# Moving the operands of an expert layer to other distances modulo 512 bytes

## The chip, the cores and the metric

One core of a Trainium2 chip runs the whole program. The metric is the device time of one execution in microseconds; a time of several runs is their median. SBUF, the on-chip memory from which TensorE reads, has 128 partitions, and a tile has one byte address that holds in each of them. "Modulo 512" below means that address modulo 512 bytes.

## The reference, cut to what matters

```python
def _attn_ref(q, k, v, s):                     # B, H, S, D = 8, 8, 576, 64
    scores = q @ k.T / sqrt(D)                 # causal, with a bias from the running sum of relu(s)
    ...
    return softmax(scores) @ v

def _moe_ref(x, modality_id, w_gate, modality_bias, w1, w2):
    e_idx = np.argmax(x @ w_gate + modality_bias[modality_id], axis=1)      # one of 8 experts a row
    ...
    for e in range(E):                         # x 4608 x 512, w1 512 x 1024, w2 1024 x 512
        mask = e_idx == e
        h = np.maximum(x[mask] @ w1[e], 0.0)
        out[mask] = gate_w[mask, None] * (h @ w2[e])
```

The output of attention, turned so that one row is one position with all heads, is the input of a layer with eight experts, of which each row uses one.

## The kernel before, in words

**Attention** (`Attn`, until about 365 us) goes through 32 pairs of heads. For each it makes score tiles from QH, QL (loaded operand) and KA, KB (streamed operand) at lines 374, 396, 409 and 410, takes exponentials, turns the tiles on TensorE against an identity (`ident`, lines 441 and 456) and multiplies with V (line 528). Its tiles lie in pools of their own, which are given back before the expert stage needs the room.

**Routing** (`Route`) writes the rows of each expert to a list in memory.

**The expert stage** (`Moe`, from about 368 us) takes blocks of 256 rows of one expert: 18 blocks by `block`, then by `two` a closing block of two 64-row pieces of different experts. For each block:

- `fetch` starts the transfer of a chunk of 512 KB of the expert's weights into a raw buffer, `wraw` (2 buffers) or `wrbw` (4 buffers); an expert has 8 chunks, four of w1 and four of w2.
- `parts` splits a chunk into a high and a low part (ScalarE or GpSimd copies the high part, VectorE or GpSimd subtracts) and writes both into a tile of 2 x 1024 columns: `wca` (4 buffers), `wcb` (5) or `wcc0` to `wcc3` (4), used in rotation.
- `gather2` loads the rows, `xt` turns them and splits them into `xT`, 2 x 4 x 256 columns, two buffers. The first block's turned rows are made during attention, in a buffer of attention's that still stands (`early_rows`), and show in the profile under the name `x`.
- `block` computes the first layer (line 1198): 96 matmuls that load 128 columns of a weight tile and stream 256 columns of `xT`. It writes the activations, split again, into `hT`. `second` computes the second layer (line 1172): 48 matmuls that load 128 columns of `hT` and stream 512 columns of a weight tile.

A matmul's loaded operand shows in the profile under PEld (LDWEIGHTS), the matmul itself under PE. TensorE takes them in the order of the program.

**Where tiles lie.** A pool gives its tiles room in the order in which their names are first asked for, and a pool begins where the one before it ends; the pool of `wcc` stands on the right side and is filled downwards from its end. `gap` asks for a tile that nothing uses; it only moves what stands after it (in the pool of `wcc`, what stands before it). The order is: `mwa` (`wraw` x2, then `wca` x4), then attention's constant tiles or, after attention, `mys` (ys), `mmx` (xr, tg, xg), `mwr` (`wrbw` x4), `mwb` (gap, `wcb` x5), `mm` (gap, three `oi` of 32 bytes, `hT` of 16384 bytes, `xT` x2 of 8192 bytes each), `mtb`. `mwa` begins at 22176, `wraw` at 160 modulo 512.

Of the kernel before, what the change touches and what calls it, by code (L numbers as in the profile page):

```python
# [8 lines left out]
F32R = mybir.dt.float32r  # L9
# [8 lines left out]
P = 128  # L18
# [643 lines left out]
class Route:  # L662
# [82 lines left out]
    def group(self, bp, x, psum, mm, then=None):  # L745
# [5 lines left out]
        for g in range(3):  # L751
            t = slice(4 * g, min(4 * g + 4, 9))
            nc.vector.tensor_reduce(out=lg[:, t].rearrange("p t (d r) -> p t d r", r=2), in_=x[g][:, :, 32:].rearrange("p t d h r -> p t d r h"), axis=AX.X, op=ALU.add)
            yield True
        nc.vector.tensor_tensor(lg, lg, self.mbs[:, 9 * bp:9 * bp + 9], ALU.add)
        mx = w.tile([P, 9], F32, name="rmx")
        nc.vector.tensor_reduce(out=mx, in_=lg, axis=AX.X, op=ALU.max)
        yield True
# [7 lines left out]
        nc.vector.scalar_tensor_tensor(oh, lg, 0.0, self.ew.unsqueeze(1).broadcast_to(B3), ALU.is_equal, ALU.mult)  # L766
        nc.vector.tensor_reduce(out=mx, in_=oh, axis=AX.X, op=ALU.max)
        gs = w.tile([P, 9], F32, name="gs")
        yield True
        ohb = self.ohb[bp % 2]  # L770
        nc.vector.tensor_tensor(ohb[:, :9], oh, mx.unsqueeze(2).broadcast_to(B3), ALU.is_equal)
        nc.vector.tensor_reduce(out=gs, in_=ex, axis=AX.X, op=ALU.add)
        for _ in range(2 if mm else 0):
# [28 lines left out]
        df = pt[:, 60:69]  # L802
        nc.vector.tensor_reduce(out=df, in_=pos, axis=AX.X, op=ALU.add)
        nc.vector.tensor_copy(di, df)
# [27 lines left out]
    def spread(self, tag, n, E, nb):  # L832
# [23 lines left out]
        def pick(v, name):  # L856
            r = cell(nb, name)
            if v is None:
                nc.vector.tensor_reduce(out=r, in_=oh, axis=AX.X, op=ALU.add)
            else:  # L860
# [123 lines left out]
class Moe:  # L984
    def __init__(self, ctx, tc, R, w1, w2, ident, out):
        self.nc, self.tc, self.R, self.w1, self.w2, self.ident, self.out = tc.nc, tc, R, w1, w2, ident, out
        self.wa = ctx.enter_context(tc.tile_pool(name="mwa", bufs=1))
        self.wb = None
        self.n = 0
        self.last = [None] * 4  # L990
        self.hold = None
        self.late, self.stop = None, 1 << 30
        self.back = ()
        self.er = None
        self.conv, self.high = [], None

    def open(self, ctx):
        tc = self.tc
        self.my, self.mx, self.wr, self.wb, self.mp = (
            ctx.enter_context(self.tc.tile_pool(name=n, bufs=2, reuse_waits="tile")) for n in ("mys", "mmx", "mwr", "mwb", "mm"))  # L1000
        self.R.tb = ctx.enter_context(tc.tile_pool(name="mtb", bufs=1, reuse_waits="tile"))
        self.ps = ctx.enter_context(tc.tile_pool(name="mps", bufs=2, space=PSUM, reuse_waits="tile"))
        self.gap(self.wb, 416)
        self.gap(self.mp, 96)

    def gap(self, pool, n):
        pool.tile([P, n // 4], F32, name="gap", bufs=1)
# [1 line left out]
    def open2(self, ctx):  # L1009
        self.wc = ctx.enter_context(self.tc.tile_pool(name="mwc", bufs=1, reuse_waits="tile", side="right"))  # L1010
        for n in ("ql", "hs"):
            self.wc.tile([P, 512], F32, name=n, bufs=2)
        for i in range(self.NC):
            self.wc.tile([P, 2, 1024], F32R, name=f"wcc{i}")
        self.gap(self.wc, 320)

    NA, NB, NC = 4, 5, 4

# [18 lines left out]
    def parts(self, raw, d, n, j, w=None):  # L1037
        nc = self.nc
        m = (n - self.NA) % (self.NA + self.NB + self.NC)
        if w is not None:  # L1040
            pass
        elif n < self.NA or self.NB <= m < self.NB + self.NA:
            w = self.wa.tile([P, 2, 1024], F32R, name="wca", bufs=self.NA)
        elif m < self.NB:
            w = self.wb.tile([P, 2, 1024], F32R, name="wcb", bufs=self.NB)
        else:
            w = self.wc.tile([P, 2, 1024], F32R, name=f"wcc{(m - self.NB - self.NA + 2) % self.NC}")
        n += 1
        with ExitStack() as after:
            for i in self.tr[1:] if 4 < n <= 8 else self.back:  # L1050
                after.enter_context(self.tc.issue_after(i.ins))
            if n <= self.NA:
                nc.gpsimd.tensor_scalar(w[:, 0], raw, 1.0, 1.0, ALU.mult, ALU.mult)
            else:
                self.high = nc.scalar.copy(w[:, 0], raw).ins
            self.conv.append((self.high, (nc.gpsimd if n in WGP else nc.vector).tensor_tensor(w[:, 1], raw, w[:, 0].bitcast(F32), ALU.subtract).ins))
        return w, d
# [19 lines left out]
    def weights2(self, es):  # L1077

        W = [], []

        def more():
            for j in range(8):
                for q in range(2):
                    w = None
                    if (j, q) == (6, 1):
                        w = self.mp.tile([P, 2, 4, 256], F32R, name="xT").rearrange("p a k n -> p a (k n)")
                    w, d = self.parts(*self.fetch(es[q], j), w)
                    W[q].append(w)
                    self.hold = d.ins
                    yield  # L1090
        return W, more()
# [48 lines left out]
    def xt(self, xg, nu):  # L1140
        nc = self.nc
        if nu < 2:
            return self.xq(xg) if nu else self.x2(xg)
        xT = self.mp.tile([P, 2, 4, 256], F32R, name="xT")
        for g in range(2):
            tp = self.ps.tile([P, 2, 256], F32, name="tp")
            tr = nc.vector.transpose(out=tp.rearrange("p k (t n) -> p k t n", n=32),
                                     in_=xg[0].rearrange("p t (d k) -> p k t d", k=4)[:, 2 * g:2 * g + 2])
            hi = nc.scalar.copy(xT[:, 0, 2 * g:2 * g + 2], tp)
            lo = nc.vector.tensor_tensor(xT[:, 1, 2 * g:2 * g + 2], tp, xT[:, 0, 2 * g:2 * g + 2].bitcast(F32), ALU.subtract)  # L1150
        self.tr = (tr, hi, lo)
        return xT
# [57 lines left out]

    def xq(self, xg):
        nc = self.nc
        xT = self.mp.tile([P, 2, 4, 256], F32R, name="xT")[:, 0, :, :P]
        tp = self.ps.tile([P, 4, 64], F32, name="tp")
        for k in range(4):
            nc.tensor.transpose(out=tp[:, k], in_=self.quads(xg[:64], k), identity=self.ident[:64, :64])
        nc.scalar.copy(xT[:, :, :64], tp)
        nc.vector.tensor_tensor(xT[:, :, 64:], tp, xT[:, :, :64].bitcast(F32), ALU.subtract)
        return xT
# [12 lines left out]

    def x2(self, xg):
        nc = self.nc
        X = self.mp.tile([P, 2, 4, 256], F32R, name="xT")[:, 0]
        tp = self.ps.tile([P, 4, P], F32, name="tp")
        for k in range(4):
            nc.tensor.transpose(out=tp[:, k], in_=self.quads(xg, k), identity=self.ident)
        self.split(X, tp)
        return X  # L1240

    def sums2(self, o, W, parts, scale=1.0, after=(), apart=False):

        nc = self.nc
        n = len(parts)
        def order(i):
            return (0, 1) if i == 0 else (1, 0)

        if apart:

            seq = [(i, c, q) for h in range(2) for q in range(2) for i in range(n // 2 * h, n // 2 * h + n // 2) for c in order(i)]
        else:
            seq = [(i, c, q) for i in range(n) for c in order(i) for q in range(2)]
        for i, c, q in seq:
            x, k, c0 = parts[i]
            m = 64 if c else P
            self.last[0] = nc.tensor.matmul(o[q][:m], x[:, P * q:P * q + m], W[q][k][:, c, c0:c0 + 512], start=i == 0 and c == 0, stop=i == n - 1 and c == 0)
        lo = self.wc.tile([P, 512], F32, name="ql", bufs=2)
        for q in range(2):
            with ExitStack() as behind:  # L1260
                for i in after:
                    behind.enter_context(self.tc.issue_after(i.ins))
                r = slice(64 * q, 64 * q + 64)
                self.last[3] = nc.scalar.activation(lo[r], o[q][64:], AF.Copy, scale=scale if type(scale) is float else scale[r])
        return lo
# [287 lines left out]
```

## Time and profile before

| | |
|---|---|
| median of the runs shown | 791.98 us (791.36 to 792.59, 2 runs) |
| the profiled execution | 791.26 us |
| its span, first to last instruction | 789.5 us |
| instructions | 17275 |
| mean granted clock of TensorE | 0.997 |
| matmuls (PE) / loads (PEld) | 5796 / 5796 |

A group of instructions is shown with its line, engine, operation, the tiles it writes and reads, its shape (loaded rows\*columns, then streamed rows x columns), its count, its busy time and the mean duration of one. Matmuls overlap in the pipeline and their ends are modelled, so the duration of one is longer than the time to the start of the next; that time is called the pitch below. A table by stretches gives, for each engine, the busy time and the number of instructions, then the granted clock, the share of the transfer engines that is busy, and GB/s.

### The profile page before, as it was taken

How to read it: one execution, taken by the hardware profiler on the slowest of the kernel's cores; microseconds unless marked ns; L12 is line 12 of the kernel's file. 1: busy time of each engine (PE TensorE's matmuls, PEld its weight loads, DVE VectorE, ACT ScalarE, POOL GpSimd, SP SyncE). 2: the span in 40 equal slices, each digit the busy share in tenths (PEclk: the TensorE clock that was granted, in tenths of full speed). 3: DMA queues.
4: the chain of work that ended last, by engine and by line, in shares of the span. 5: the costliest groups of instructions: out<-in, count | busy, mean ns of one | idle time of the engine just before them, and what ended most of it. 6: DMA issues, size and time to landing. Idle time of an engine off the chain costs nothing. (4 is left out here: it accounts for less than half of the span.)

```text
span 789.5 us, 17275 instructions
## 1 busy us (share of the span) xinstructions
PE 774.3 (98%) x5796; PEld 673.1 (85%) x5796; DVE 568.3 (72%) x1440; ACT 518.4 (66%) x1163; POOL 367.1 (46%) x386
## 2 busy tenths in 40 slices
PE   7999999999999999998999999999999999999996
PEld 6888788888888888887888999999999998999984
DVE  7675577665766666777689797877777776778664
ACT  6887878878888778884455445655555555455553
POOL 8978877898789978994610101110000011001011
PEclk9999999999999999999999999999999999999999
DMA  7467556776567765757888979877788787887750
GB/s 241 132 225 224 186 191 190 216 249 215 157 185 236 230 194 155 233 181 237 272 305 278 329 240 335 241 266 243 244 265 270 256 245 249 267 264 266 269 171 29
DMA packets 88168, 181.21 MB, mean 230 GB/s; under 512 B 13785, under 2 KB 33113, under 8 KB 87950
## 3 DMA queue, kind: packets, MB, share of 16 engines
q1 hardware_dynamic: 82238, 160.03, 65.1%
q0 software_dynamic: 5840, 20.06, 6.6%
q8 instruction: 46, 0.75, 0.4%
q14 instruction: 44, 0.36, 0.2%
HBM read 143.59 MB, written 26.80 MB: 216 GB/s over the span
## 5 line engine op out<-in xcount | busy, mean ns | idle before, releaser
L1184 POOL DMA_INDIRECT out<-ys,oi x36 | 40.8, 1132 | 339.5 <-ACT ys L1183 245.8
L421 ACT ACTIVATE pe<-pe,mx 128x512 f32<-128x512 f32 (+3 forms) x256 | 142.4, 559 | 11.7 <-DVE mx L398 11.6
L398 DVE CUSTOM_DVE_ANT_0 pe<-sp,mk 128x512 f32<-128x512 f32 (+3 forms) x256 | 116.6, 481 | 43.2 <-ACT rs L538 20.2
L445 ACT COPY PT<-pt 128x512 f32<-128x512 f32 (+1 forms) x192 | 94.3, 504 | 27.4 <-PE pt L441 26.4
L441 PE MATMUL pt<-ident,pe 128*128 128x128 f32 x640 | 106.1, 278 | 0.9 <-ACT PT L445 0.7
L374 PE MATMUL sp<-KA,QH 128*128 128x256 f32 (+2 forms) x256 | 98.1, 388 | 1.8 <-POOL KA L238 1.8
L1200 ACT ACTIVATE hT<-hp 128x512 fp32r<-128x512 f32 x72 | 43.1, 599 | 85.2 <-PE hp L1198 85.0
L328 POOL TENSOR_TENSOR QL<-rawq,QH 64x576 fp32r<-64x576 f32 x62 | 87.0, 1422 | 0.3
L328 POOL TENSOR_TENSOR KA<-rawk,KA 64x576 fp32r<-64x576 f32 x62 | 86.4, 1412 | 0.1
L1198 PE MATMUL hp<-xT,wcb 128*128 128x256 f32 x648 | 86.1, 277 | 0.0
L441 PEld LDWEIGHTS pt<-ident,pe 128*128 128x128 f32 x640 | 77.2, 144 | 9.0 <-ACT PT L445 2.0
L396 PE MATMUL sp<-KB,QL 76*128 76x256 f32 (+2 forms) x256 | 83.8, 329 | 1.1 <-DMA KB<-KA 0.9
L528 PE MATMUL o<-PT,V 128*64 128x512 f32 (+1 forms) x496 | 84.5, 440 | 0.0
L1198 PEld LDWEIGHTS hp<-xT,wcb 128*128 128x128 f32 x648 | 79.9, 188 | 0.8 <-DVE hT L1201 0.2
L1201 DVE SCALAR_TENSOR_TENSOR hT<-hp,hT 128x512 fp32r<-128x512 f32 x72 | 49.5, 687 | 41.8 <-ACT hT L1200 41.4
L1172 PE MATMUL y<-wcb,hT 128*128 128x512 f32 x336 | 79.3, 392 | 0.0
L1172 PEld LDWEIGHTS y<-wcb,hT 128*128 128x128 f32 x336 | 62.5, 188 | 13.1
L1198 PE MATMUL hp<-xT,wca 128*128 128x256 f32 x528 | 72.3, 277 | 0.0
L1198 PEld LDWEIGHTS hp<-xT,wca 128*128 128x128 f32 x528 | 66.0, 188 | 0.7 <-DVE hT L1201 0.2
L528 PEld LDWEIGHTS sp<-PT,V 128*64 128x64 f32 x620 | 38.2, 137 | 33.3 <-issue 28.8
L1198 PE MATMUL hp<-xT,wcc 128*128 128x256 f32 x456 | 63.0, 277 | 1.1 <-DVE hT L1201 1.1
L1172 PE MATMUL y<-wca,hT 128*128 128x512 f32 x264 | 62.3, 392 | 0.0
(300 smaller groups left out, 1688.0 us busy)
## 6 DMA issues: line engine op xcount, KB each, us to landing
wrbw<-in_w SPq DMA_DIRECT2D x104, 512.0 KB
wraw<-in_w SPq DMA_DIRECT2D x56, 512.0 KB
rawq<-in_qkv SPq DMA_DIRECT2D x31, 576.0 KB
rawk<-in_qkv SPq DMA_DIRECT2D x31, 576.0 KB
V<-in_qkv SPq DMA_DIRECT2D x32, 320.0 KB
KB<-KA SPq DMA_DIRECT2D x62, 144.0 KB
xr<-lists SPq DMA_DIRECT2D x68, 128.0 KB
lists<-z SPq DMA_DIRECT2D x8, 576.0 KB
```

The lines of the kernel that those rows point to most:

```text
L328: self.last = nc.gpsimd.tensor_tensor(o, i, h, ALU.subtract).ins
L374: self.pe.append(self.nc.tensor.matmul(sp[:, :nn], QH[:, q0:q0 + P], self.KA[u][:, ab, :nn], start=True, stop=False).ins)
L396: self.pe.append(nc.tensor.matmul(sp[:, :nn], QL[:EXT, q0:q0 + P], KB[:EXT, ab, :nn], start=False, stop=True).ins)
L398: ins = nc.vector.tensor_tensor_reduce(out=t[:, :n], in0=sp[:, :n], in1=self.mk[:, 512 - n:512], scale=-0.125, scalar=3.0e38, op0=ALU.add, ...
L421: self.act = nc.scalar.activation(t[:, :n], t[:, :n], AF.Exp, bias=m, scale=-1.0, accum_out=st["sums"][:, o:o + 1]).ins
L441: self.pe.append(nc.tensor.transpose(out=pt[:, o:o + P], in_=pe[:, P * j:P * j + P], identity=self.ident).ins)
L445: return cp(w[:, :, :, v:v + P], pt[:, :n * (1 + both)].rearrange("p (a j q) -> p a j q", a=1 + both, q=P))
L528: m = nc.tensor.matmul(t[r, q0 - b:q1 - b], V[:, ab, j, :], PT[:, ab, PTS * j + q0 if j < 4 else PTW - 64:PTS * j + q1 if j < 4 else PTW], ...
L1172: self.last[0] = nc.tensor.matmul(y[u], hT[:, a, f, P * u:P * u + P], W[4 + f // 2][:, c, 512 * (f % 2):512 * (f % 2) + 512], start=f == 0 ...
L1198: nc.tensor.matmul(hp[:, u], W[k][:, a, f:f + P], xT[:, c, k], start=k == 0 and i == 0, stop=k == 3 and i == 2)
L1200: hi = nc.scalar.activation(hs, hp, AF.Relu)
L1201: lo = nc.vector.scalar_tensor_tensor(hT[:, 1, 2 * m:2 * m + 2], hp, 0.0, hs.bitcast(F32), ALU.max, ALU.subtract)
```

## The change

Every tile of the expert stage that TensorE reads is moved:

- a gap of 224 bytes before the first `wca`, which also moves everything behind the pool `mwa` by 224 bytes;
- the gap before `wcb` grows from 416 to 480 bytes;
- the gap ahead of `hT` grows from 96 to 192 bytes;
- the gap in the pool of `wcc` grows from 320 to 384 bytes;
- `xT` becomes a tile of 2176 columns (8704 bytes), and the 2048 columns in use begin at column 32 or at column 40, in turn, that is 128 or 160 bytes into the tile.

```diff
@@ Moe.__init__
+        self.nx = 0
@@ Moe.open
-        self.gap(self.wb, 416)
-        self.gap(self.mp, 96)
+        self.gap(self.wb, 480)
+        self.gap(self.mp, 192)
+
+    def turned(self):
+        t = self.mp.tile([P, 2176], F32R, name="xT")
+        self.nx += 1
+        o = 32 + 8 * (self.nx % 2)
+        return t[:, o:o + 2048].rearrange("p (a k n) -> p a k n", a=2, k=4)
@@ Moe.open2
-        self.gap(self.wc, 320)
+        self.gap(self.wc, 384)
@@ Moe.parts
         elif n < self.NA or self.NB <= m < self.NB + self.NA:
+            if n == 0:
+                self.gap(self.wa, 224)
             w = self.wa.tile([P, 2, 1024], F32R, name="wca", bufs=self.NA)
@@ Moe.weights2
-                        w = self.mp.tile([P, 2, 4, 256], F32R, name="xT").rearrange("p a k n -> p a (k n)")
+                        w = self.turned().rearrange("p a k n -> p a (k n)")
@@ Moe.xt (and likewise xq and x2)
-        xT = self.mp.tile([P, 2, 4, 256], F32R, name="xT")
+        xT = self.turned()
```

The number and the order of the instructions in the source, their shapes and their buffers' counts are the same.

More of the change, by code (lines that the diff above doesn't have):

```diff
@@ L1212, in xq @@
         nc = self.nc
-        xT = self.mp.tile([P, 2, 4, 256], F32R, name="xT")[:, 0, :, :P]
+        xT = self.turned()[:, 0, :, :P]
         tp = self.ps.tile([P, 4, 64], F32, name="tp")
@@ L1234, in x2 @@
         nc = self.nc
-        X = self.mp.tile([P, 2, 4, 256], F32R, name="xT")[:, 0]
+        X = self.turned()[:, 0]
         tp = self.ps.tile([P, 4, P], F32, name="tp")
```

## The prediction

> **What bounds the kernel now.** I read the page from the top: busy times first, then the slices.
>
> ```profile
> PE 774.3 (98%) x5796; PEld 673.1 (85%) x5796; DVE 568.3 (72%) x1440; ACT 518.4 (66%) x1163; POOL 367.1 (46%) x386
> PE   7999999999999999998999999999999999999996
> ```
>
> TensorE is busy from the second slice to the last but one. The table by stretches confirms it for the expert stage (420 to 740 us), and the list of TensorE's waits says how little is left to win by ending a wait:
>
> ```profile
> 420.00:740.00 320.00, 318.91 (x2091) 289.50 (x2091) 249.49 (x334) 176.69 (x226) 32.57 (x29) 1.00 0.82 263
> ...
> PE hp L1198 <- DVE hT L1201: 1.9, 3, 0.9
> PE sp L374 <- POOL KA L238: 1.8, 1, 1.8
> ```
>
> 318.91 of 320 us are busy at a granted clock of 1.00 (third column from the end), and the longest wait sums to 1.9 us over the whole span. No row in that list waits for a weight or for a turned row. So this stage's length is the number of its matmuls times their pitch, the time from one start to the next. Only something that alters the pitch, or makes an operand late, can move the end.
>
> The pitch is read from the timeline, which merges neighbours: start, length, group, count. One whole expert block, with the end of the block before it:
>
> ```profile
> 447.49 0.84 PE L1198 MATMUL hp<-xT,wcc 128*128 128x256 f32 x6
> 448.17 5.66 PE L1172 MATMUL y<-wcc,hT 128*128 128x512 f32 x24
> 453.66 5.66 PE L1172 MATMUL y<-wcb,hT 128*128 128x512 f32 x24
> 459.15 1.21 PE L1198 MATMUL hp<-xT,wcb 128*128 128x256 f32 x9
> ...
> 470.06 2.22 PE L1172 MATMUL y<-wca,hT 128*128 128x512 f32 x9
> ```
>
> The 48 second-layer matmuls start from 448.17 to 459.15: 10.98 us, 228.8 ns each. The 96 first-layer matmuls start from 459.15 to 470.06: 10.91 us, 113.6 ns each. A block is 21.9 us and there are 18. By line, with shortest, median and longest duration:
>
> ```profile
> L1198 PE MATMUL hp<-xT,wcb x648: 276/276/384, 392.3 to 755.7; 128*128 128x256 f32 x162
> L1198 PE MATMUL hp<-xT,wca x528: 276/276/385, 392.6 to 756.0; 128*128 128x256 f32 x176
> L1198 PE MATMUL hp<-xT,wcc x456: 276/276/384, 414.5 to 734.1; 128*128 128x256 f32 x152
> L1198 PE MATMUL hp<-x,wca x96: 276/276/384, 368.1 to 381.2; 128*128 128x256 f32 x96
> L1172 PE MATMUL y<-wcb,hT x336: 388/392/400, 381.3 to 745.0; 128*128 128x512 f32 x168
> L1172 PE MATMUL y<-wca,hT x264: 388/392/477, 403.5 to 764.7; 128*128 128x512 f32 x132
> L1172 PE MATMUL y<-wcc,hT x264: 388/392/394, 406.2 to 767.4; 128*128 128x512 f32 x132
> ```
>
> These are 1728 first-layer and 864 second-layer matmuls. A duration here is the pitch plus a fixed tail: 276 - 113.6 = 162 and 392 - 228.8 = 163 ns. So durations can be compared across lines as pitches. Price of a nanosecond: 1728 + 864 = 2592 matmuls, 2.6 us.
>
> **The change part by part.** It adds no instruction and removes none; tiles move. I add up the sizes in order of allocation. Before, all weight tiles (wca, wcb, wcc) begin at 160 modulo 512 bytes, and hT, xT and the first block's turned rows at 352. Every column offset used (128 or 256 floats) is a multiple of 512, so in the first layer the streamed operand lies 192 past the loaded one, and in the second 320. After: wca 160 + 224 = 384; wcb 160 + 224 + 64 = 448; wcc 64 lower, 96; hT 448 + 96 + 192 = 736, that is 224; xT's data at 224 + 128 = 352 and 224 + 160 = 384 in turn. The distances become 480 and 0 (wca), 416 and 448 (wcb), 256 and 288 (wcc) in the first layer, 160, 224 and 384 in the second: nine, so it does what it says.
>
> *First and second layer.* What does a distance cost? The weights of the next matmul load while this one streams, so the pair to judge is one matmul's streamed and the next one's loaded operand. At the joints of a block other tiles meet. The last first-layer matmul streams xT (352) while hT (352) loads: distance 0. The six starts from 447.49 to 448.17 take 0.68 us, 113.3 ns each, that joint included, against 113.6 at 192. The last y streams a chunk while the next chunk loads, again 0, inside the 228.8. So distance 0 costs less than the timeline's 10 ns rounding in a joint, and the shortest and median durations give no line a second level.
>
> The attention scores meet other distances: within a row of QH, KA, QL, KB these are 0, 64, 128, 256 and 384, with a little of 192 and 320 where another line follows.
>
> ```profile
> L410 PE MATMUL sp<-KB,QL x128: 292/297/442, 15.8 to 353.1; 76*128 76x288 f32 x128
> L456 PE MATMUL pt<-ident,pep x128: 270/273/330, 21.5 to 359.3; 128*128 128x128 f32 x128
> ```
>
> L410 (64, 256 and 384) has shortest and median 5 ns apart: one level again. L456 turns tiles in two buffers 2304 bytes apart, so it sees 32 and 288 already, and its shortest and median are 270 and 273: no second level. L410's pitch is 297 - 163 = 134 ns for 288 columns, 0.465 a column, where the first layer has 113.6 / 256 = 0.444. That is the one sign in the trace that another distance may be dearer; those matmuls also use 76 rows and wait for and release other engines. 160, 224, 416, 448 and 480 are not judged by any of these rows.
>
> If halving the loaded operand shortened the pitch, the load and the stream would be in each other's way. In the closing block the same line does both:
>
> ```profile
> L1257 PE MATMUL hp<-wcc,hT 128*64 128x512 f32 x6 | 2.4, 393 | 0.0
> L1257 PE MATMUL hp<-wcc,hT 128*128 128x512 f32 x6 | 2.4, 392 | 0.0
> ```
>
> 393 ns with 64 columns before, 392 with 128: at 320 there is nothing to win. I cost the pitch at nothing. Bounds: below, every matmul at its line's shortest, 392 - 388 = 4 ns on 864, and 0 on the first layer, whose median is its shortest: -3.5 us. Above, all at L410's price a column: (0.465 - 0.444) x 256 = 5.4 ns x 1728 = 9.3 us, and for the second layer (0.465 x 512 - 228.8) = 9.3 ns x 864 = 8.0 us, +17.3 us together. I take 0, the value nearest to the joints, which are these same lines.
>
> By the Trainium skill's page "TensorE: Matmul & The Clock Gate", section "Back-to-back issue gap", a warm gap would be N / 2.4 + 2.5, which is 109.2 and 215.8 ns; by that figure an estimate of 4.4 x 1728 + 13.0 x 864 = 18.8 us could be won at most, and the trace stands above it everywhere.
>
> *Splitting, turning, raw weights.* ACT, DVE and POOL read and write moved tiles. The two raw buffers stand at different distances from the chunk (wraw 0, wrbw 96) before:
>
> ```profile
> L1056 DVE TENSOR_TENSOR wca<-wraw,wca x16: 1211/1218/1227, 387.5 to 762.2; 128x1024 fp32r<-128x1024 f32 x16
> ...
> L1056 DVE TENSOR_TENSOR wca<-wrbw,wca x32: 1198/1219/1228, 388.6 to 767.9; 128x1024 fp32r<-128x1024 f32 x32
> ```
>
> 1218 and 1219 ns: no price. What hides it if there is one: TensorE's list holds no wait for a chunk, and DVE is busy 249 of 320 us; 70 us of slack for some 130 such operations, half a microsecond each.
>
> *Transfers.* wrbw moves from 256 to 480 modulo 512, xr from 160 to 384; wraw stays at 160. Waits of the converting engines for each, before:
>
> ```profile
>   DMA wraw<-in_w: 2.5, 4
> ...
>   DMA wrbw<-in_w: 1.7, 2
> ```
>
> 56 chunks to 160 and 104 to 256 waited 2.5 and 1.7 us in all, and no matmul behind them did. Cost 0; bound: the stage's transfer share of 0.82 could rise by a fifth before transfers set the pace.
>
> The Trainium skill's page "DMA: Bandwidth & Descriptors", section "How a descriptor splits into AXI transactions", speaks against this part: a piece that does not begin on 256 bytes needs a transaction more. By it wrbw's 4096-byte rows would need 17 in place of 16, an estimate of 6% on 104 of 160 chunks, a share near 0.85, and still no matmul late, so the sum is the same by both.
>
> *Attention.* Its tiles all move by 224, so their mutual distances stay; only the identity (unmoved) meets pe at 320 instead of 32, and L456 shows two such distances alike. 0, bound 3 ns on 800 turnings, 2.4 us.
>
> *Sum.* 0. The profiled execution took 791.26 us for a span of 789.5, 1.8 around it; the median shown is 791.98. I predict 792.0.
>
> **The rivals.**
>
> *A load that no longer hides (slower).* At wca's distances, 0 and 480, load and stream run over nearly the same addresses modulo 512; if they excluded each other, the load would come on top. The price is read from the turnings, where a 128-column stream is too short to hide a load:
>
> ```profile
> 200.33 0.60 PE L441 MATMUL pt<-ident,pe 128*128 128x128 f32 x4
> ```
>
> 0.60 less the last one's 0.272, over 3, is 109 ns, against 57 for half of a first-layer matmul: 52 ns exposed. On half of wca's 528 (distance 0), 13.7 us: 806. On all 528 and the first block's 96, 32 us: 824. It decides from 300 matmuls on, where 52 ns make 15.8 us. Against it: the joint at 0. For it: a joint is one matmul in 96, and 480 is unseen.
>
> *All distances but 192 and 320 are dearer.* L410's price: 809; half of it: 800.
>
> *Faster.* The nine distances could remove part of what stretches the matmuls. The rows alone give -3.5 us, 788.5; the whole of the skill's gap would be 773. Against it: the 64-column rows.
>
> *It does not do what it says.* The pools could round or order tiles otherwise than I added up; then some distances stay and the time is 792 again.
>
> **How the numbers follow.** No change, 788 to 796: 0.70. Addresses otherwise, also 792: 0.05. All dearer, 797 to 809: 0.13, a fifth of it past 2%. Load exposed, 806 to 824: 0.08, four fifths of it past 2%. Faster: 0.04, of which 0.02 past 2%. A kernel's measurement tells about 2% (15.8 us) from no change. Faster by over 2%: 0.02; slower by over 2%: 0.03 + 0.06 = 0.09; the rest, 0.89, within. The range goes from 786, under the rows' bound of 788.5, to 807, under the top of the dearer case; most of the exposed case stays out.
>
> **What would show it.** Right: L1198 at 276 and L1172 at 392 median for all of wca, wcb and wcc, and the stretch 420 to 740 with about 2091 matmuls. Exposed load: wca's median in L1198 near 300 or in two levels, wcb's and wcc's unmoved. All dearer: 282 and 401 in all lines. Late weights: TensorE waits for a chunk, which it now never does. Wrong beyond that: a level at 160 or 224 in the second layer, where no row warned.

## The result, and the profile after

The changed kernel takes 802.52 us (801.90 to 803.15, 2 runs) against 791.98: a ratio of 1.0132, 95% interval 1.0114 to 1.015. The profiled execution took 801.9 us for a span of 800.2, 10.7 us longer than before's 789.5. Ratios here and below are of fast executions alone, which leaves out one of e2's four, at 1972.08 us. The top of the page after:

```profile
PE 785.7 (98%) x5796; PEld 681.3 (85%) x5796; DVE 569.3 (71%) x1440; ACT 518.3 (65%) x1163; POOL 364.6 (46%) x386
```

PE's busy time rose by 11.4 us for the same 5796 matmuls and that of their loads by 8.2; DVE, ACT and POOL moved by 2.5 us at most. The table by stretches says where (busy time and count of PE, PEld, DVE, ACT, POOL, then granted clock, transfer share, GB/s):

```profile
0.00:368.00 368.00, 360.50 (x3114) 300.97 (x3114) 249.02 (x1008) 290.22 (x869) 312.14 (x339) 1.00 0.65 204
368.00:420.00 52.00, 51.88 (x333) 47.25 (x334) 39.08 (x61) 27.62 (x41) 15.39 (x13) 0.97 0.86 264
420.00:740.00 320.00, 319.15 (x2049) 288.32 (x2048) 246.96 (x331) 171.43 (x220) 31.73 (x29) 1.00 0.80 261
```

In the expert stretch TensorE is as busy as before (319.15 us) and gets 2049 matmuls done in place of 2091, at a clock of 1.00 in both. It is not waiting; each matmul is longer. The transfer share fell from 0.82 to 0.80 with the pace. The 0.97 in the second row is a stretch of 3.4 us at half clock, about 1.7 us of time; the profiles below have none, one or two such stretches there, and before's other executions range from 0.992 to 0.999 in mean granted clock, so I don't count it into the change's price.

By line, with shortest, median and longest duration:

```profile
L1207 PE MATMUL hp<-xT,wcb x648: 276/281/287, 393.8 to 766.1; 128*128 128x256 f32 x162
L1207 PE MATMUL hp<-xT,wca x528: 274/282/302, 394.1 to 766.4; 128*128 128x256 f32 x176
L1207 PE MATMUL hp<-xT,wcc x456: 274/281/384, 416.4 to 743.9; 128*128 128x256 f32 x152
L1207 PE MATMUL hp<-x,wca x96: 277/281/588, 369.1 to 382.4; 128*128 128x256 f32 x96
L1181 PE MATMUL y<-wcb,hT x336: 388/395/398, 382.6 to 755.0; 128*128 128x512 f32 x168
L1181 PE MATMUL y<-wca,hT x264: 390/397/479, 405.2 to 775.2; 128*128 128x512 f32 x132
L1181 PE MATMUL y<-wcc,hT x264: 387/393/408, 408.0 to 778.0; 128*128 128x512 f32 x132
```

The median of the first layer went from 276 to 281 or 282 for every weight tile, that of the second from 392 to 393, 395 and 397. The timeline shows it as pitch:

```profile
449.88 0.87 PE L1207 MATMUL hp<-xT,wcc 128*128 128x256 f32 x6
450.59 5.73 PE L1181 MATMUL y<-wcc,hT 128*128 128x512 f32 x24
456.16 5.76 PE L1181 MATMUL y<-wcb,hT 128*128 128x512 f32 x24
461.75 1.22 PE L1207 MATMUL hp<-xT,wcb 128*128 128x256 f32 x9
```

48 starts from 450.59 to 461.75 are 11.16 us, 232.5 ns each (228.8 before); the six from 449.88 are 0.71 us, 118 ns each (113.3 before). The list of TensorE's waits holds nothing new in the expert stage; its one row there is:

```profile
PE hp L1207 <- DVE hT L1210: 0.7, 1, 0.7
```

Adding up the time from each start to the next over all recorded matmuls: first layer 199.3 to 206.6 us (+7.3), second layer 198.5 to 201.8 (+3.4), everything else 391.8 and 391.8. So the whole loss lies in the two lines whose operands moved.

To judge each distance I matched the recorded starts to the program's matmuls with their two addresses (streamed operand of one, loaded operand of the next) and took the mean of start to next start within a layer:

| layer | before | after, by distance |
|---|---|---|
| first, 256 columns | 192: 113.8 ns | 0: 119.3; 256: 118.8; 288: 117.0; 416: 118.3; 448: 116.1; 480: 118.3 |
| second, 512 columns | 320: 229.1 ns | 160: 234.1; 224: 233.1; 384: 232.5 |

Weighted by count that is +4.1 ns on 1728 and +4.2 ns on 864: 7.1 + 3.6 = 10.7 us. (The half clock adds 1.7 us to the first layer; shorter waits for hT, 1.9 to 0.7 us, take 1.2 from it; that the sum meets the span to a tenth is partly chance.) All nine are dearer, and over these distances the two layers pay about the same per matmul.

### The profile page after: what moved, and what is told of

It reads as the page before. It is cut to its first block, busy times and chain, and to the rows that moved or that the text cites. A ratio compares the mean times of both kernels' runs of the same rounds, so it can differ in the third digit from the quotient of the medians.

```text
span 800.2 us, 17275 instructions
## 1 busy us (share of the span) xinstructions
PE 785.7 (98%) x5796; PEld 681.3 (85%) x5796; DVE 569.3 (71%) x1440; ACT 518.3 (65%) x1163; POOL 364.6 (46%) x386
## 5 line engine op out<-in xcount | busy, mean ns | idle before, releaser
L1193 POOL DMA_INDIRECT out<-ys,oi x36 | 39.1, 1086 | 350.8 <-ACT ys L1192 256.9
L1207 PE MATMUL hp<-xT,wcb 128*128 128x256 f32 x648 | 88.1, 280 | 0.0
L1207 PEld LDWEIGHTS hp<-xT,wcb 128*128 128x128 f32 x648 | 81.8, 188 | 0.6
L1207 PE MATMUL hp<-xT,wca 128*128 128x256 f32 x528 | 74.9, 282 | 0.0
L1207 PEld LDWEIGHTS hp<-xT,wca 128*128 128x128 f32 x528 | 68.4, 190 | 0.5
L1207 PE MATMUL hp<-xT,wcc 128*128 128x256 f32 x456 | 64.8, 281 | 0.8 <-DVE hT L1210 0.7
```

The costliest lines, as they stand in the source:

```text
L1207: nc.tensor.matmul(hp[:, u], W[k][:, a, f:f + P], xT[:, c, k], start=k == 0 and i == 0, stop=k == 3 and i == 2)
```

## The experiments

All edits are against the kernel before. Where xT moves within its tile (not in e1, and otherwise in e4), it does so by the change's own function with one start column for both buffers:

```diff
+    def turned(self):
+        t = self.mp.tile([P, 2176], F32R, name="xT")
+        o = ...                                # the column given with the experiment
+        return t[:, o:o + 2048].rearrange("p (a k n) -> p a k n", a=2, k=4)
```

**Is it the place or the distance?** e1_all_moved moves weights (to 384), xT and hT (to 64), the first block's rows and the raw buffer wrbw (to 480) and keeps the distances at 192 and 320.

```diff
+            if n == 0:
+                self.gap(self.wa, 224)
-        self.gap(self.wc, 320)
+        self.gap(self.wc, 96)
-        xT = b[:, 32:2080]...
+        xT = b[:, 88:2136]...
```

> Every expert tile is moved as far as or further than in the change (weights 160 to 384, turned rows and hT 352 to 64, wrbw 256 to 480, attention's tiles by 224), but all distances stay at 192 and 320. Theory D (the pitch depends on the distance between the streamed and the loaded operand alone): 792 us, first layer 113.8 ns, second 229.1 ns a matmul. Rival A (where an operand itself lies, or the moved raw buffers and their transfers, cost the time): about 801 us, pitches near 118 and 233. Rival V (it is the variety of distances, not their values): 792 us.

Measured: 791.76 us, ratio 0.9987 (0.9977 to 0.9997). Its row of the stretches and two of its groups (busy time and mean ns behind the bar):

```profile
420.00:740.00 320.00, 318.91 (x2092) 289.43 (x2091) 249.93 (x334) 176.84 (x226) 33.06 (x29) 1.00 0.82 264
```

```profile
L1200 PE MATMUL hp<-xT,wcb 128*128 128x256 f32 x648 | 85.9, 277 | 0.0
...
L1174 PE MATMUL y<-wcb,hT 128*128 128x512 f32 x336 | 79.2, 391 | 0.0
```

2092 matmuls in the stretch against 2091, 277 and 391 ns. Absolute places, transfers into a raw buffer at 480, splitting and turning cost nothing that shows; if anything the kernel is 1 us faster. The Trainium skill's page "DMA: Bandwidth & Descriptors", section "How a descriptor splits into AXI transactions", would by the prediction's reading have given wrbw's rows one transaction more (the page tells it of the bytes that a transaction fetches, and wrbw is written). The share stands at 0.82 with wrbw at 480 as at 256.

**Distance 0 in the first layer alone.** e2_first_zero: start column 80, so xT lies at 160 like the weights, and the first block's rows likewise. The second layer stays at 320.

```diff
+        o = 80
-        xT = b[:, 32:2080]...
+        xT = b[:, 112:2160]...
```

> The turned rows alone are moved, to 160: all first-layer matmuls have distance 0, the second layer stays at 320. Theory D: the first layer goes to the 119.3 ns that distance 0 has in the changed kernel, 5.5 x 1728 = +9.5 us, 801 to 802 us; second layer unmoved at 229. Rival V (one distance for all is cheap whatever it is) and the reading of the joints in the prediction (distance 0 costs nothing): 792 us, 113.8 ns.

Measured: 802.98 us (median of the other three executions), ratio 1.0125 (1.0099 to 1.0151).

```profile
L1205 PE MATMUL hp<-xT,wcb 128*128 128x256 f32 x648 | 89.9, 283 | 0.0
...
L1179 PE MATMUL y<-wcb,hT 128*128 128x512 f32 x336 | 79.2, 391 | 0.0
```

The first layer's pitch is 119.9 ns (+6.1 on 1728 matmuls, 10.5 us), the second's 229.0, unmoved. A long run at distance 0 is dear, though a single pair at 0, from the first to the second layer in before's joints, is not (113 to 114 ns in 20 of 21).

**Distance 160 in the second layer alone.** e3_second_160: the gap ahead of hT 96 to 256, start column 88, which leaves xT at 352.

```diff
-        self.gap(self.mp, 96)
+        self.gap(self.mp, 256)
+        o = 88
```

> hT alone is moved, to 0: all second-layer matmuls have distance 160, the first layer stays at 192. Theory D: second layer 234.1 ns, 5.0 x 864 = +4.3 us, 796 us, first layer 113.8. Rival V: 792 us, 229.1 ns.

Measured: 801.38 us, ratio 1.0102 (1.008 to 1.0124).

```profile
L1205 PE MATMUL hp<-xT,wcb 128*128 128x256 f32 x648 | 87.9, 280 | 0.0
...
L1179 PE MATMUL y<-wcb,hT 128*128 128x512 f32 x336 | 80.9, 396 | 0.0
```

The second layer came out at 234.0 ns. But the first layer rose too, to a mean of 116.5, at the distance of 192 that it had before. Its timeline shows two levels, in blocks as a whole:

```profile
440.45 0.85 PE L1205 MATMUL hp<-xT,wca 128*128 128x256 f32 x6
...
451.34 5.77 PE L1179 MATMUL y<-wcc,hT 128*128 128x512 f32 x24
...
462.58 1.22 PE L1205 MATMUL hp<-xT,wcb 128*128 128x256 f32 x9
...
473.88 8.59 PE L1179 MATMUL y<-wca,hT 128*128 128x512 f32 x36
```

From 440.45 to 451.34 the 96 matmuls take 113.4 ns each, from 462.58 to 473.88 117.7 ns, with the same operands' distance, in the same line. So a distance has no single price; at least two patterns of it exist.

The trace of before held the same two levels, in one block:

```profile
418.92 1.18 PE L1198 MATMUL hp<-xT,wcb 128*128 128x256 f32 x9
...
421.24 0.62 PE L1198 MATMUL hp<-xT,wcc 128*128 128x256 f32 x3 [0.22 <-DVE hT L1201]
421.69 1.22 PE L1198 MATMUL hp<-xT,wcb 128*128 128x256 f32 x9
...
431.67 5.76 PE L1172 MATMUL y<-wca,hT 128*128 128x512 f32 x24
```

Behind a wait of 0.22 us, 48 matmuls at 192 settled at 117.8 ns, where the 48 ahead of it had 113.3, and the second layer behind them, at 320, settled at 233.4 in place of 228.9. These 92 matmuls of 2592 show in no line's shortest or median duration.

**A third of the first layer.** e4_low_half moves only the low half of xT by 320 bytes, so that behind the first block one first-layer matmul in three has distance 0.

```diff
+        t = self.mp.tile([P, 2304], F32R, name="xT")
+        return t[:, :2208].rearrange("p (a z) -> p a z", a=2)[:, :, :1024]...
```

> Only the low half of each block's turned rows is moved by 320 bytes: of three first-layer matmuls in a row, the third streams at distance 0, the other two at 192. Theory D with each matmul for itself: 5.5 x 1632 / 3 = +3.0 us, 795 us, pitch 119 after a low half and 114 after a high one. If a single matmul at another distance is absorbed by its neighbours (as the joints of a block before suggest): 792 us, 114 for all. Rival V: all three rise, to 117 to 119, near 800 us.

Measured: 801.74 us, ratio 1.011 (1.0089 to 1.013), nearly the price of moving all.

```profile
L1205 PE MATMUL hp<-xT,wcb 128*128 128x256 f32 x648 | 88.8, 281 | 0.0
...
L1179 PE MATMUL y<-wcb,hT 128*128 128x512 f32 x336 | 80.1, 395 | 0.0
```

The matmuls at 0 took 119.4, those still at 192 117.8, and the second layer at 320 fell into two levels (229 and 233, mean 231.1). In those blocks, past their first starts, the matmuls at 192 ran at 116.7 ns in some blocks and 119.4 in others, never at the 113.3 or 117.8 that they have by themselves. So matmuls at one distance change the pace of their neighbours at another.

**Matmuls alone.** m1_only_matmuls runs only matmuls, with no transfer and no wait within a set: 24 of 256 and of 512 columns at each distance in steps of 16 bytes; then 12 of 512 columns at a distance d followed at once by 36 of 256 at 192 (tiles on); then the same with a break between the two (tiles br). ScalarE copies a finished result out, in the breaks where there is one and during the next set where there is none. m2_loads_and_entries goes by 8 bytes, repeats 256 columns with loads of 64 columns in place of 128 (h), and enters six distances by 8 matmuls of 512 columns at six others (y):

```python
for d in TRIED:                    # 64, 112, 192, 320, 368, 448
    for e in BEFORE:               # 0, 64, 96, 128, 160, 224
        ...
        second(o, Y[e], 8)         # 8 x 512 columns at distance e
        first(p, X[d], 24)         # 24 x 256 columns at distance d
        ...
```

> Not the layer: matmuls of the same shapes alone (load 128 columns, stream 256 or 512, float32r), nothing else running meanwhile, output meaningless. First 24 matmuls of 256 columns at each distance from 0 to 496 in steps of 16, then 24 of 512 columns at each, with a break before each set; then, for 16 distances, 12 of 512 columns at that distance followed at once by 36 of 256 columns at 192 (tiles on...), and the same with a break between (tiles br...). Theory D (distance alone): 256 columns 113.8 ns at 192, 119 at 0, 119 at 256, 118 at 416 and 480, 117 at 288, 116 at 448; 512 columns 229 at 320, 234 at 160, 233 at 224 and 384; all on and br sets 113.8. Theory P (load and stream settle into a repeating pattern, which also depends on how the run was entered, as the third experiment suggests): br sets 113.8, on sets 113.8 after some distances and about 117.7 after others, after 160 among them. Rival O (the other engines' accesses to the same addresses cost the time): the same pitch at all distances, 113.8 and 229.

> Matmuls alone again, output meaningless. First 256 columns at every distance in steps of 8; then the same with 64 instead of 128 columns loaded (tiles h...); then 24 matmuls at 64, 112, 192, 320, 368 or 448, entered without a break from 8 matmuls of 512 columns at 0, 64, 96, 128, 160 or 224. Theory P (load and stream meet in SBUF and settle into a repeating pattern): the levels repeat after 256 bytes; with half the load the dear distances lose part of their 4 to 7 ns over 113; a good distance gives 113.3 after some entries and 117.8 after others. Rival D (one level for each distance): 113.3 after every entry, 117.8 at 320 after every entry. Rival S (the stream alone has trouble where it begins in SBUF): no change with half the load.

m1's timeline, two of its entries, and two of the sets at 192 behind a break:

```profile
391.85 4.24 PE L41 MATMUL p<-on128s,S 128*128 128x256 f32 x36
395.93 2.97 PE L41 MATMUL o<-d160s,S 128*128 128x512 f32 x12
398.73 4.40 PE L41 MATMUL p<-on160s,S 128*128 128x256 f32 x36
402.97 2.97 PE L41 MATMUL o<-d192s,S 128*128 128x512 f32 x12
...
510.90 4.51 PE L41 MATMUL o<-br128s,S 128*128 128x256 f32 x36 [0.73 <-ACT res L48]
...
580.94 4.36 PE L41 MATMUL o<-br384s,S 128*128 128x256 f32 x36 [0.73 <-ACT res L48]
```

36 matmuls at 192 take 4.08 us (113.3 each) when matmuls at 128 ran before them, and 4.24 us (117.8 each) after 160. The sets without a break agree for every two preceding distances that are 256 apart, and m2 gives the same answer for each of its six entries into 192. Behind a break theory P expected 113.8 throughout, and that failed: seven of the sixteen br sets settled at 117.8 and nine at 113.3, and three times two distances 256 apart differ (128 and 384 above). So the matmuls ahead choose the pattern where a run goes on without a pause, and something that no run here isolates chooses it behind a pause. While a set behind a break ran, nothing else did on the core: both the price and the two patterns are TensorE's own. m2's timeline:

```profile
83.32 3.36 PE L43 MATMUL o<-d104s,S 128*128 128x256 f32 x24 [0.52 <-ACT res L50]
87.19 3.02 PE L43 MATMUL o<-d112s,S 128*128 128x256 f32 x24 [0.52 <-ACT res L50]
...
200.16 3.36 PE L43 MATMUL o<-d360s,S 128*128 128x256 f32 x24 [0.52 <-ACT res L50]
204.03 3.02 PE L43 MATMUL o<-d368s,S 128*128 128x256 f32 x24 [0.52 <-ACT res L50]
...
269.82 2.95 PE L43 MATMUL o<-h0s,S 128*64 128x256 f32 x24 [0.52 <-ACT res L50]
...
290.97 3.07 PE L43 MATMUL o<-h192s,S 128*64 128x256 f32 x24 [0.51 <-ACT res L74]
```

104 and 360 agree, 112 and 368 agree, and of the 31 pairs 256 apart that ran at full clock 30 settle within half a nanosecond of each other (the other, 160 and 416, at 119.0 and 117.1; 0 and 256 are left out, since 0 ran mostly at half clock). In m1's sweep nine of fifteen do; 64 and 320 lie furthest apart, at 113.3 and 117.8, and m2 has both at 117.8. So what counts is the distance modulo 256, not 512, and several distances have more than one level. The settled pitch, over the later starts of a set, goes from 113.3 ns (112) to 130.0 (104), 126.7 at 8, 120.0 at 256. For 512 columns m1 settled at 226.7 at 0 and 256, 229.0 at 64 and 320, 234.2 at 160, 233.3 at 224 and 384. With 64-column loads 0 is among the cheap ones (113.3) and 192 among the dear (119.2). The entries of m2:

```profile
356.16 2.92 PE L43 MATMUL p<-d112s,S 128*128 128x256 f32 x24
358.92 2.00 PE L43 MATMUL o<-y64s,S 128*128 128x512 f32 x8
...
383.86 2.99 PE L43 MATMUL p<-d192s,S 128*128 128x256 f32 x24
386.68 2.01 PE L43 MATMUL o<-y64s,S 128*128 128x512 f32 x8
...
393.23 2.89 PE L43 MATMUL p<-d192s,S 128*128 128x256 f32 x24
395.96 2.03 PE L43 MATMUL o<-y128s,S 128*128 128x512 f32 x8
```

At 192 the set takes 2.82 us to the next start behind y0 and 2.73 behind y96. At 192 and 448 only the entries by 96 and 128 settled at 113.3, at 64 only those by 160 and 224; at 112 and 368 all six did.

**What the bench promises, in the kernel.** Four layouts bring the second layer to 0 or 256, where the bench has 226.7 ns. The gap ahead of hT and the start column:

```diff
-        self.gap(self.mp, 96)
+        self.gap(self.mp, 416)   # v1, v3, v4: second layer at 0; v2: 160, second layer at 256
+        o = 48                   # v1, xT stays at 352; v2: 112, likewise; v3: 16, first layer at 64; v4: 28, first layer at 112
```

(v3 and v4 move the first block's rows to the same place.)

> hT moves to 160, so the second layer has distance 0; the first layer stays at 192. From matmuls alone: second layer 226.7 ns, (229.1 - 226.7) x 864 = -2.1 us. Theory D: first layer 113.8, so 790 us. Theory P: the first layer is entered otherwise than before, and takes 113.4 (790 us) or 117.8 ns (+6.9 us, 797 us), or one in some blocks and the other in others.

> The same with hT at 416, distance 256 in the second layer. Theory D: 226.8 ns there, 790 us. Theory P: 226.8 to 230.8 in the second layer (matmuls alone showed both), first layer 113.4 or 117.8: 790 to 799 us.

> hT at 160 (second layer 0) and the turned rows at 224 (first layer 64). In matmuls alone 64 was at 113.3 from its first matmul. Theory D: 113.3 and 226.7, 789 to 790 us. Theory P: the same, if 64 settles into its good pattern from every entry; 797 us if not.

> hT at 160 (second layer 0) and the turned rows at 272 (first layer 112, which settled at 113.3 ns from all seven entries with matmuls alone). Theory P: first layer 113.4, second 226.8 ns, against 113.8 and 229.1 before: -0.4 x 1728 - 2.3 x 864 = -2.7 us, 789 us. Theory D: the same, since matmuls alone gave 113.3 at 112. Rival O (other engines disturb the good pattern in the kernel, as they may have done at 64): first layer near 117.6, 796 us.

| run | distances | us | ratio (95%) | first, second pitch, ns |
|---|---|---|---|---|
| v1_second_0 | 192, 0 | 796.41 | 1.0054 (1.004 to 1.0068) | 117.5, 226.8 |
| v2_second_256 | 192, 256 | 796.17 | 1.0053 (1.004 to 1.0066) | 117.5, 226.8 |
| v3_first_64 | 64, 0 | 797.02 | 1.007 (1.0056 to 1.0083) | 117.7, 227.5 |
| v4_first_112 | 112, 0 | 791.31 | 0.9992 (0.9983 to 1.0002) | 114.0, 227.4 |

Theory D is out: at the same 192 the first layer is dear in nearly every block of v1 and v2. In v3 the distance 64, at 113.3 in m1's sweep, settled at 117.8 in every whole block. v1's timeline around one second layer:

```profile
449.08 0.87 PE L1205 MATMUL hp<-xT,wcc 128*128 128x256 f32 x6
449.79 5.60 PE L1179 MATMUL y<-wcc,hT 128*128 128x512 f32 x24
455.23 5.60 PE L1179 MATMUL y<-wcb,hT 128*128 128x512 f32 x24
460.67 1.22 PE L1205 MATMUL hp<-xT,wcb 128*128 128x256 f32 x9
```

48 matmuls from 449.79 to 460.67: 226.7 ns, 2.1 less than before, worth 1.8 us. But the first layer, at its old 192, goes on in the dear pattern (0.71 us for six) and gives back more than three times as much (3.7 ns on 1728 matmuls, 6.4 us). v4 puts the first layer where every entry settled:

```profile
L1205 PE MATMUL hp<-xT,wcb 128*128 128x256 f32 x648 | 85.8, 276 | 0.0
...
L1179 PE MATMUL y<-wcb,hT 128*128 128x512 f32 x336 | 78.7, 390 | 0.0
```

276 and 390 ns: the first layer is cheap behind a second layer at 0. Its starts add up to 200.8 and 197.0 us, 397.8 against before's 397.7 (a stretch of 3.4 us at half clock is in the 200.8); the time can't be told from before's. The 2.7 us that were expected did not come: behind the first block each first layer settled at 113.3, but its first starts are dearer, so that the mean is 114.0, and by the two means only 1.1 us could be won.

**Was it hT's place?** In e3, hT had moved, and its writers with it. v5_112_after_160 is e3 with xT, and the first block's rows, at 112 past the weights.

```diff
-        self.gap(self.mp, 96)
+        self.gap(self.mp, 256)
+        o = 68
-        xT = b[:, 32:2080]...
+        xT = b[:, 12:2060]...
```

> The third experiment (hT at 0, second layer 160) with one thing changed: the turned rows at 272, so that the first layer has 112 in place of 192. Theory P: 112 settles into its good pattern after the second layer at 160 too, where 192 did so in some blocks only: first layer 113.5 in place of 116.5 ns, second unmoved at 234, so 5 us less than the third experiment, 796 us. Rival: what raised the first layer there was hT's new place and the writes to it, not the entry: 116.5, 801 us.

Measured: 798.11 us, ratio 1.0074 (1.0055 to 1.0094), 3.3 us under e3 (2.2 by the two ratios, each against its own runs of before), where 5 were expected.

```profile
L1205 PE MATMUL hp<-xT,wcb 128*128 128x256 f32 x648 | 86.0, 276 | 0.0
...
L1179 PE MATMUL y<-wcb,hT 128*128 128x512 f32 x336 | 81.0, 396 | 0.0
```

With hT where e3 had it and the second layer still at 160 (234.3 ns), the first layer is back at 276 (114.3 ns against 116.5). So hT's place and the writes to it do not by themselves make a first layer slow; e3's own blocks at 113.4, with hT in the same place, say the same.

## Why the prediction was right or wrong

*The number.* 792.0 was 10.5 us too low, and the case called most likely, 788 to 796 at 0.70, did not come. 802.52 lies inside 786 to 807 only because the range took in a rival that was given 0.13.

*What bounds the kernel.* Right: the stage's length is count times pitch, durations are the pitch plus a fixed tail (281 - 118 = 163 again), and no wait entered the sum.

*The nine distances.* The addresses came out as added up, so "it does not do what it says" is out.

*The pitch, costed at nothing.* This step failed, at "distance 0 costs less than the timeline's 10 ns rounding in a joint". The reading was right: single pairs at 0 do run at 113 ns. The inference from one pair to a run of them was not: e2 shows 119.9 ns when all are at 0, and m1, m2 and e4 show that the pace at a distance depends on the matmuls before. That one pair in 96 rides in the pattern of its neighbours fits this, but no run tests one pair alone. "The shortest and median durations give no line a second level" was true and hid two things in the same trace: the block at 421 us, and the first five starts of nearly every first layer, which take 116 to 123 ns before it settles at 113. The price was 7.1 + 3.6 us in place of 0.

*The two checks on attention's rows.* L456's two distances, 32 and 288, are 256 apart, and the bench repeats after 256 bytes, so that they were alike says nothing. L410 meets 448 besides the three distances listed: 31 of its 128 matmuls stand ahead of a load of V. L410's 0.465 ns a column, "the one sign in the trace that another distance may be dearer", pointed the right way and was put aside. As an upper bound it held: +9.3 and +8.0 us against 7.1 and 3.6. That is luck: as a rate by columns it failed (4.1 ns at 256 columns, 4.2 at 512), and in the bench a distance of 256 costs 6.7 ns over the best at 256 columns and nothing at 512.

*64 columns against 128.* "At 320 there is nothing to win" stood at 320. That load and stream are then not in each other's way did not follow: with 64-column loads other distances are the dear ones (m2), and at 0 the second layer runs at 226.7 ns, 2.1 under before's.

*Transfers, splitting, attention.* Each at nothing was right: e1 moves these tiles too and takes 791.76 us; all but the two layers is 391.8 us before and after; no matmul waits for a chunk.

*The rivals.* "All distances but 192 and 320 are dearer", at "half of it: 800", is what happened to the time, but not its reason: 192 itself goes to 117.8 in e3 and v1, and 0 in the second layer is cheaper than 320. Its sign, 282 in all lines of the first layer, came; its 401 in the second was too much (393 to 397). The exposed load did not come: wca at distance 0 is at 282, not near 300, and 480 at 118.3 ns. The warning of a level at 160 or 224 that no row showed was right (234.1 and 233.1), but they were not alone. The faster case did not come: all nine are dearer, and the lowest settled pitches of any run, 113.3 and 226.7 ns, stay above the prediction's 109.2 and 215.8; v4, which settles at both, can't be told from before.

*A rule of the notes.* The Trainium skill, "SBUF — State Buffer", section "Who interferes with whom", gives the streamed operand and LDWEIGHTS a read port each and says "PE and ACT never wait on anyone". In m2's sweep, with nothing else at work during a set, the pitch still goes from 113.3 to 130.0 ns by the distance of these two reads alone; the measurement decides.

What stays open: what in the reads makes the patterns, what chooses one behind a pause, why 64-column loads shift them, and which entry the kernel's own joints amount to. In the bench 192 settles at 117.8 behind 12 matmuls at 320; in the kernel before, where 320 also comes ahead but other tiles meet in the joint, it settles at 113.6. So the bench does not foretell a kernel's pattern at a distance that has two, such as 192 or 64; at 112, which settled alike from every entry tried, its answer carried over.

## What to carry to other kernels

In a stretch where TensorE is busy throughout, the distance between streamed and loaded operand is worth 4 to 6 ns a matmul, 10 us of 792 here, and no wait, engine or transfer shows it: compare durations and counts in a stretch. Judge a distance by a long run at it, entered in several ways, never by a single pair in a joint. Prefer one that settles at the low pitch from every entry (112 modulo 256 for 128-column loads and 256-column streams, of the three that were entered in several ways here: 64, 112 and 192) over one that is as fast only behind the right neighbour.

## What the runs showed of the hardware that was not expected

- The pitch of dense matmuls depends on the two operands' distance modulo 256 bytes: 113.3 to 130.0 ns for 256 columns, 226.7 to 236.7 for 512, at a granted clock of 1.00 (m1, m2; e1 shows that it is the distance and not the place).
- One distance can have two steady paces, kept for a whole block: 113.3 or 117.8 ns at 192 (m1, m2, e3, one block of before), 229 or 233 at 320 (e4, the same block). Without a pause the matmuls before choose which (m1, m2); behind a pause both came (m1).
- Moving one matmul in three slows the others as well (e4: a mean of 117.8 at the unmoved 192, settled at 116.7 or 119.4).
- Moving raw buffers, turned rows and activations without changing the distances changes nothing that shows (e1: ratio 0.9987).
